# Attention feeding a SwiGLU block: six edits of order in the first 150 microseconds

## The chip, the cores and the metric

The kernel runs on one core of a Trainium2 chip. The time is the device time of one execution in microseconds, given as the median of several runs; less is better. Engines are named as in the profile: PE (TensorE, matmuls), PEld (its weight loads), DVE (VectorE), ACT (ScalarE), POOL (GpSimd) and SP (SyncE, which issues transfers). Each engine runs its own instructions in the order in which they are written, and waits for others through semaphores. A transfer is issued by one engine and lands later, on the 16 DMA engines.

## What is computed

```python
# q, k, v: (8, 12, 448, 64)
scores = scale * np.matmul(q, k.transpose(0, 1, 3, 2))
attn   = softmax(scores)                       # over the last axis
x      = np.matmul(attn, v)                    # (8, 12, 448, 64)
x      = x.transpose(0, 2, 1, 3).reshape(3584, 768)
g      = x @ w_gate                            # (768, 1536)
val    = x @ w_val
out    = (g * sigmoid(g) * val) @ w_out        # (3584, 768)
```

So there are 96 attention heads, taken as 48 pairs (0 to 47), six pairs to a batch entry, and then a gated feed-forward block over 3584 tokens.

## The kernel before

**Pairs.** A pair goes through these stages: its q and k are loaded (`load_qk16`, issued by POOL) and turned to `qkT`; its scores are computed in units (`qk`, PE into a two-bank score tile `s`), exponentiated by ACT into `E`; its v is loaded (`load_v`, POOL) and copied by DVE into `vo` (`copy_v`, L189); the products with v go to `acc` (`pv`, L354/L362 for pairs 0 to 11, L389 for later ones); DVE divides by the sums (R, L373/L414, and xt, L375/L415); and `turn_x` brings xt into X, on PE for pairs 0 to 11 (L447, with a DVE cast at L454), by transposing transfers afterwards.

The turning of q and k changes with the pair: up to pair 10 it is done on PE (`turn`, L262 to L272, 18 transposes into a tile `tp` and a DVE copy); from pair 11 (`NPE`) on POOL copies the raw values (L208) and SP issues two transposing transfers (L210 and L214). `QUAD` is 12: from pair 12 on, scores are cut in another way (L298 for whole units, L310 for the unit RU that two pairs share). `FIRST` is 6 and `WIDE` is 8.

**Feed-forward.** Tokens are cut into blocks, two to a pair of batch entries: even ones with 384 tokens, odd ones with 512. Each block has 12 steps. A step (class `Step`) has six gate matmuls (L519 into `gp`), ACT's Tanh (L544), DVE's `t` (L567), six value matmuls (L519 into `vp`) and DVE's `hts` (L572), the input of the output products. The output products follow: for blocks 0 and 1 plain ones (L606), for later ones groups that use seven products in place of eight (`out_group`, L635), which need sums of weights (L491 to L494, `wsums`, 12 DVE operations) and of `hts` (L502 to L505). The sums wait in a list, `sums`, and `add_sum` issues them one by one at places written by hand.

**PSUM.** There are two rings: `ps_s`, three tiles of two banks, for scores, gates and groups, and `ps_f`, two tiles of one bank, for products, turned values, value matmuls and plain outputs. A gate takes the first bank of a `ps_s` tile and keeps the second as `spare`; in a *bare* visit (below) it takes a `ps_f` tile instead (`gate_small`).

**Order.** The order on each engine is the order in which the code issues instructions. After the first 24 units of scores, the code walks through `plan`, a list of visits. A visit has two or three units of scores (two up to unit 32, three afterwards) and the pairs whose products are due (`todo`). A visit in which none is due is *bare*. In a visit, in this order: the scores; early v copies; for each pair entered, `lead`, the pairs whose copy and transposes (`prep`) are issued, then the loads of a pair 6 further on and of the v of a pair 3 further on; the products; then the v copies of the pairs due in the next visit; then feed-forward work, as much as `run_budget` gives (the time left, over the visits left, plus what was carried); then the turns of the pairs of this visit. `run_budget` takes single steps (`run_fv`), output products (`run_o`) or, in odd blocks, two steps at a time (`run_pair`). In `run_pair` both gates come first, then the first step's value matmuls, then the second step's, in two halves of 256 columns (`split`): the first half goes to `spare`, the bank beside the second step's own gate, so the scheduler lets it start only when `t` of that step has read the gate. From block 2 on, the visits follow the lists `EVEN` and `ODD`.

The early entries to know: entering pair 9 issues the copies of pairs 12 and 13 on POOL; entering pair 10 issues that of pair 14, entering 11 that of pair 15, and entering 10 also the loads of pair 16 and of v of pair 13.

The step 0 of block 0 has one more peculiarity: the sixth of its six input parts comes from the pair 5, whose turn (`late`) is put inside the step, between the first five gate matmuls and the first five value matmuls.

Lines that the change and the prediction touch: `turn` L262, `gate` L527, `value` L547, `run_fv` L800, `run_pair` L811, `run_o` L836, `run_group` L845, `run_budget` L867, `lead` L989, `carry` L1021.

Of the kernel before, what the change touches and what calls it, by code (L numbers as in the profile page):

```python
# [10 lines left out]
FP32 = mybir.dt.float32  # L11
# [12 lines left out]
FIRST = 6  # L24
WIDE = 8
# [7 lines left out]
QUAD = 12  # L33
# [6 lines left out]
def kernel(  # L40
# [16 lines left out]
    NCB = DM // 128  # L57
# [31 lines left out]
    ps_f = ctx.enter_context(tc.tile_pool(name="ps_f", bufs=2, space=PSUM))  # L89
# [129 lines left out]
    def prep(pr):  # L219
        if pr >= QUAD:  # L220
            return prep_quad(pr)
        rq, rk = raw[pr]
        if pr == 0 or pr >= NPE:
            qk16 = attp.tile([128, 2, NC, 2, D], FP16, tag="qk16", name="qk16", bufs=3)[0:P]
            for t, src in enumerate((rq, rk)):
                dst = qk16[:, 1 - t].rearrange("p c h d -> p h c d")
                if pr == 0:
                    nc.vector.tensor_copy(dst[:, 0], src[:, 0])
                    nc.scalar.activation(dst[:, 1], src[:, 1], AF.Copy)
                else:  # L230
                    nc.gpsimd.tensor_copy(dst, src)
        qkT[pr] = attp.tile([128, 2 * S + D], FP16, tag="qkT", name="qkT", bufs=QB)
        if pr >= NPE:
            nc.sync.dma_start_transpose(
                qkT[pr][:, 0 : 2 * S].rearrange("p (c q) -> p c q", q=P),
                qk16.rearrange("p t c h d -> p (t c h d)"),
            )
            nc.sync.dma_start_transpose(
                qkT[pr][:, 2 * S :].rearrange("p (c q) -> p c q", c=1),
                qk16[0:D, 1, 0].rearrange("p h d -> p (h d)"),  # L240
            )
            return None

        def turn0():
            for t in range(2):
                tp = ps_s.tile([128, 2, 512], FP32, tag="s", name="tp")
                for c in range(NC):
                    for hx in range(2):
                        nc.tensor.matmul(
                            tp[ts(hx, 64), c // 2, ds(c % 2 * P, P)],  # L250
                            lhsT=qk16[:, 1 - t, c, hx],
                            rhs=ident[0:P, 0:P],
                            start=True,
                            stop=True,
                        )
                dst = qkT[pr][:, ts(1 - t, S)].rearrange("p (a x) -> p a x", a=2)
                nc.vector.tensor_copy(dst[:, 0], tp[:, 0, 0 : 2 * P])
                nc.scalar.activation(dst[:, 1], tp[:, 1, 0 : 2 * P], AF.Copy)
                if t == 0:
                    nc.vector.tensor_copy(qkT[pr][:, 2 * S :], tp[:, 0, 0:D])  # L260

        def turn():  # L262
            if pr < FIRST + 3:
                tp = ps_s.tile([128, 2, 1024], FP16, tag="s", name="tp")[:, 0]
            else:
                tp = ps_f.tile([128, 1024], FP16, tag="f", name="tp")
            for i in range(2 * NC + 1):
                t, c = (1 - i // NC, i % NC) if i < 2 * NC else (0, 0)
                for hx in range(2):
                    src = raw[pr][t][:, hx, c, :]  # L270
                    nc.tensor.transpose(tp[ts(hx, 64), ts(i, P)], src, ident[0:P, 0:P])
            nc.vector.tensor_copy(qkT[pr][:], tp[:, 0 : 2 * S + D])  # L272

        return turn if pr else turn0
# [207 lines left out]
    gate_small = [False]  # L482
# [25 lines left out]
    class Step:  # L508
# [18 lines left out]
        def gate(self):  # L527
            n = self.at[2]
            if gate_small[0]:
                gate_small[0] = False  # L530
                gp = ps_f.tile([128, 512], FP32, tag="f", name="gp")
            else:
                gs = ps_s.tile([128, 2, 512], FP32, tag="s", name="gp")
                gp, self.spare = gs[:, 0], gs[:, 1]
            if self.late:
                self.vp = ps_f.tile([128, 512], FP32, tag="f", name="vp")
                self.group("g", gp, range(NCB - 1))
                self.late()
                self.group("v", self.vp, range(NCB - 1))
                self.group("g", gp, [NCB - 1])  # L540
            else:
                self.group("g", gp, range(NCB))
            self.sg = fp.tile([128, 512], FP32, tag="sg", name="sg")
            nc.scalar.activation(self.sg[:, 0:n], gp[:, 0:n], AF.Tanh, scale=0.5)  # L544
            self.gp = gp
# [157 lines left out]
    with tc.manual_schedule():  # L703
# [91 lines left out]
        def add_sum(n=1):  # L795
            for _ in range(n):
                if sums:
                    sums.pop(0)()

        def run_fv(quiet=False):  # L800
            step = fvq.pop(0)
            step.gate()
            step.value(0)
            if not quiet:
                add_sum()
            step.finish()
            if not quiet:
                add_sum()
            return 2 * step.time

        def run_pair(small=0):  # L811
            one, two = fvq.pop(0), fvq.pop(0)
            two.split = two.at[2] == 512
            one.gate()
            two.gate()
            one.value(0)
            one.gated()
            if small:
                add_sum()
            two.gated()  # L820
            one.finish()
            two.value(0)
            if not small:
                add_sum()
            two.finish()
            return 4 * one.time
# [9 lines left out]
        def run_o():  # L836
            gen, t = oq.pop(0)
            next(gen)
            if len(oq) < 2 and not groups and wsums:
                sums.extend(wsums[:3])  # L840
                wsums[:3] = []
                add_sum(3)
            return t

        def run_group(nf, inside=None, gate_first=False):  # L845
            gen = groups.pop(0)[0](gate_first)
            for _ in range(nf - 1):
                run_fv()
            step = fvq.pop(0)
            if gate_first:  # L850
                step.gate()
                add_sum()
            next(gen)
            if not gate_first:
                step.gate()
                add_sum()
            if inside:
                inside()
                next(gen)
            step.value(0)  # L860
            add_sum()
            step.finish()
            if not inside:
                next(gen)
            add_sum()

        def run_budget(budget):  # L867
            while (fvq or oq) and budget > 0:
                if not fvq:
                    budget -= run_o()  # L870
                elif len(fvq) > 1 and fvq[0].at[1] and 2 * fvq[0].time < budget <= 4 * fvq[0].time:
                    budget -= run_pair(1)
                else:
                    budget -= run_fv()
            return budget

        def left():
            return sum(2 * step.time for step in fvq) + sum(t for _, t in oq)
# [77 lines left out]
        for x, (chunks, todo) in enumerate(plan):  # L956
# [29 lines left out]
                copy_v(p0)  # L986
            entered = [pr for pr, c in chunks if c == 0]
            for pr in entered:
                lead = [pr + 3] if pr + 3 < QUAD else [pr + 3, pr + 4] if pr + 3 == QUAD else [pr + 4]  # L989
                for p in lead:  # L990
                    if NPE <= p < NPAIR:
                        prep(p)
                if 14 <= pr + LA < NPAIR:
                    load_qk16(pr + LA, 1)
                if 12 <= pr + 3 < NPAIR:
                    load_v(pr + 3)
# [18 lines left out]
            if adds[max(y for y in adds if y <= x)] < 2:  # L1015
                if bare and oq and not fvq:
                    carry -= run_o()
                elif bare:
                    gate_small[0] = True
                out_small[0] = not fvq and bool(oq) and any(p0 >= QUAD for _, p0 in todo)  # L1020
                carry = run_budget(left() / (end - x) + carry)  # L1021
            else:
                nf, ng, no = steps.pop(0) if steps else (0, 0, 0)
                gate_small[0] = bare
                after_group = ng > 0
                if ng:
                    run_group(nf, gate_first=bare)
                    nf = 0
                if no or bare_next(x):
                    for _ in range(nf):  # L1030
                        run_fv()
                else:
                    run_steps(nf)
                for _ in range(no):
                    run_o()
# [55 lines left out]
```

## Time and profile before

| what | before |
|---|---|
| median of 3 runs | 440.3 us (440.25 to 440.62) |
| the profiled execution | 440.02 us |
| its span | 438.3 us |
| PE busy | 429.2 us (98%) |
| DVE, ACT, POOL busy | 260.7, 222.6, 183.0 us |
| PE busy from 0 to 130 us | 125.16 us |
| granted TensorE clock | 1.00 |

The span is the time between the first and the last instruction of the profiled execution; the execution lasts 1.7 us longer. A line of the timeline gives the start and the length in microseconds, the engine, the line of the code, the operation, the tiles that it writes and reads, their shapes, how many instructions it joins, and in brackets the idle time ahead of it with what ended it. On PE the matmuls overlap, so the length of a group has the filling of the array in it, and an idle time in brackets is less than the time lost. At full clock a matmul passes 2.4 columns per ns: one of 384 columns takes 0.16 us, one of 512 takes 0.21.

### The profile page before, as it was taken

To read this page: it belongs to the slowest core of one execution; us is meant where nothing else is said; L and a number is where in the kernel's file an instruction comes from. 1 tells how busy PE (TensorE), PEld (TensorE's weight loads), DVE (VectorE), ACT (ScalarE), POOL (GpSimd) and SP (SyncE) were. 2 spreads that over 40 slices of the span, in tenths; PEclk is the share of its full clock that TensorE was granted. 3 is DMA by queue.
4 is the path that set the end of the run, shared out by engine and by line. 5 is a ranking of instruction groups with operands and counts; after the bars stand their busy time and mean duration, and the time that the engine had idled before them with its cause. 6 is when DMAs were issued, how large, how long until landed. Compare 5 with 4: busy or idle time off the path is not lost.

```text
span 438.3 us, 11082 instructions
## 1 busy us (share of the span) xinstructions
PE 429.2 (98%) x4488; PEld 277.1 (63%) x4488; DVE 260.7 (59%) x604; ACT 222.6 (51%) x332; POOL 183.0 (42%) x301
## 2 busy tenths in 40 slices
PE   8999999999999999999999999999999999999996
PEld 3665556554556676674656676674756778566486
DVE  4666662667668656755456755664556765654562
ACT  6975667546554645464645454546464542222221
POOL 8755624998796446546433553723000000000000
PEclk9999999999999999999999999999999999999999
DMA  9999999999999697965797679964152012202015
GB/s 138 183 199 200 198 175 174 141 159 227 142 144 109 83 167 110 173 81 78 120 140 111 81 125 135 145 103 72 34 107 56 12 30 75 75 2 72 2 36 147
DMA packets 108436, 49.98 MB, mean 114 GB/s; under 512 B 60832, under 2 KB 105024, under 8 KB 108384
## 3 DMA queue, kind: packets, MB, share of 16 engines
q0 software_dynamic: 46928, 24.75, 47.5%
q1 hardware_dynamic: 61296, 24.32, 28.6%
q8 instruction: 35, 0.57, 0.5%
q10 hardware_dynamic: 160, 0.20, 0.1%
q14 instruction: 17, 0.14, 0.1%
HBM read 49.55 MB, written 11.01 MB: 138 GB/s over the span
## 4 chain that ended last, share of the span: by engine, by line
PE 75%; DMA 15%; POOL 4%; DVE 2%; ACT 2%; issue 1%; SPq 0%; DVEq 0%; POOLq 0%
PE gp L519 22%; PE vp L519 19%; PE og L635 17%; PE acc L389 8%; DMA qkraw<-in_k_dram 6%; PE s L298 5%; DMA wg<-in_moe_w_gate_dram 4%; PE op L606 3%; DMA qkraw<-in_q_dram 3%; POOL qkraw L171 2%; DMA qkT<-qk 1%; PE s L310 1%; DVE t L567 1%; ACT E L318 1%; ACT sg L544 1%
## 5 line engine op out<-in xcount | busy, mean ns | idle before, releaser
L318 ACT ACTIVATE E<-s 128x896 f16<-128x896 f32 x126 | 106.6, 918 | 33.5 <-PE s L298 20.2
L519 PE MATMUL gp<-X,wg 128*128 128x384 f16 (+1 forms) x576 | 123.3, 353 | 0.0
L519 PE MATMUL vp<-X,wv 128*128 128x384 f16 (+2 forms) x576 | 120.8, 347 | 0.0
L544 ACT ACTIVATE sg<-gp 128x384 f32<-128x384 f32 (+1 forms) x96 | 52.4, 546 | 89.6 <-PE gp L519 85.2
L567 DVE SCALAR_TENSOR_TENSOR t<-sg,gp 128x384 f32<-128x384 f32 (+1 forms) x96 | 59.5, 620 | 63.4 <-ACT sg L544 62.6
L519 PEld LDWEIGHTS <-wv 128*128 128x128 f16 x606 | 59.2, 98 | 51.6 <-issue 2.0
L519 PEld LDWEIGHTS <-wg 128*128 128x128 f16 x576 | 53.6, 98 | 45.6 <-issue 2.4
L208 POOL COPY qk<-qkraw 128x512 f16<-128x512 f16 x72 | 44.4, 655 | 88.3 <-DMA qkT<-qk 87.7
L572 DVE SCALAR_TENSOR_TENSOR hts<-t,vp 128x384 f16<-128x384 f32 (+2 forms) x96 | 58.2, 607 | 9.9 <-PE vp L519 2.0
L596 POOL DMA_DIRECT2D out_dram<-osb x2 | 1.1, 552 | 131.5 <-DVE osb L688 131.5
L148 POOL DMA_DIRECT2D vraw<-in_v_dram x72 | 44.2, 641 | 9.1 <-DMA wo<-in_moe_w_out_dram 7.5
L148 POOL DMA_DIRECT2D qkraw<-in_k_dram x70 | 42.5, 624 | 6.9 <-DMA wo<-in_moe_w_out_dram 5.6
L635 PEld LDWEIGHTS <-hts 128*128 128x128 f16 x528 | 44.0, 98 | 1.3 <-issue 0.3
L389 PEld LDWEIGHTS <-E 128*128 128x128 f16 (+1 forms) x1152 | 37.4, 96 | 11.1 <-issue 4.6
L336 ACT ACTIVATE E<-s 112x896 f16<-112x896 f32 x48 | 40.7, 917 | 7.3 <-PE s L328 7.1
L389 PE MATMUL acc<-vo,E 128*128 128x65 f16 (+1 forms) x1152 | 42.2, 192 | 0.2 <-DVE hts L572 0.2
L654 ACT ACTIVATE osb<-og 128x384 f32<-128x384 f32 x22 | 10.8, 490 | 44.8 <-PE og L635 40.8
L414 DVE RECIPROCAL R<-acc 128x4 f32<-128x4 f32 x72 | 12.8, 178 | 33.5 <-PE acc L389 33.5
L415 DVE TENSOR_TENSOR xt<-acc,R 128x256 f16<-128x256 f32 x72 | 30.6, 425 | 2.7 <-DMA qkT<-qk 0.3
L171 POOL DMA_DIRECT2D qkraw<-in_q_dram x44 | 30.0, 681 | 3.8 <-DMA wg<-in_moe_w_gate_dram 1.0
L298 PE MATMUL s<-qkT 64*128 64x448 f16 x216 | 30.0, 353 | 0.2 <-DVE t L567 0.2
L635 PE MATMUL og<-wo,hts 128*128 128x192 f16 x264 | 29.0, 246 | 0.0
(81 smaller groups left out, 417.5 us busy)
## 6 DMA issues: line engine op xcount, KB each, us to landing
vraw<-in_v_dram POOLq DMA_DIRECT2D x72, 64.0 KB, 4.3
qkraw<-in_q_dram POOLq DMA_DIRECT2D x41, 112.0 KB, 4.2
qkraw<-in_k_dram POOLq DMA_DIRECT2D x68, 64.0 KB, 4.4
wg<-in_moe_w_gate_dram POOLq DMA_DIRECT2D x8, 288.0 KB, 9.4
wv<-in_moe_w_val_dram POOLq DMA_DIRECT2D x8, 288.0 KB, 10.4
wo<-in_moe_w_out_dram POOLq DMA_DIRECT2D x2, 1152.0 KB, 19.8
out_dram<-osb SPq DMA_DIRECT2D x7, 288.0 KB, 4.1
out_dram<-osb SPq DMA_DIRECT2D x6, 336.0 KB, 4.1
```

What stands on the lines that cost most here:

```text
L148: eng.dma_start(dst[ts(s, 64)], rows)
L171: nc.gpsimd.dma_start(dst, flat.rearrange("h (p c) d -> p h (c d)", c=NC))
L208: nc.gpsimd.tensor_copy(dst.rearrange("p c h d -> p h c d"), src)
L298: nc.tensor.matmul(s[:, hx, 0:S], lhsT=t[ts(hx, 64), ts(c + low(pr, hx), 128)], rhs=t[ts(hx, 64), ds(NC * 128, S)], start=True, stop=True,)
L318: nc.scalar.activation(e[:, 0 : 2 * S].rearrange("p (h q) -> p h q", h=2), s[:, :, 0:S], AF.Exp, scale=sm_scale)
L336: nc.scalar.activation(e[:, :, 0:S], s[0:P, :, 0:S], AF.Exp, scale=sm_scale)
L389: nc.tensor.matmul(acc[:, ts(j, D + 1)], lhsT=e[rows, ds(hx * S + j * 128, 128)], rhs=Vts[pr % NV][rows, hx, col, 0 : D + 1], start=first, ...
L519: nc.tensor.matmul(dst[:, 0:w], lhsT=wslice(kind, self.fb, cb), rhs=X[kk][:, cb, ds(c0 + lo, w)], start=(cb == 0), stop=(cb == NCB - 1),)
L544: nc.scalar.activation(self.sg[:, 0:n], gp[:, 0:n], AF.Tanh, scale=0.5)
L567: nc.vector.scalar_tensor_tensor(self.t1[:, 0:n], self.sg[:, 0:n], 1.0, self.gp[:, 0:n], ALU.add, ALU.mult)
L572: nc.vector.scalar_tensor_tensor(self.hts[:, self.fb, ds(lo, w)], self.t1[:, ds(lo, w)], 0.5 * HS, vp[:, 0:w], ALU.mult, ALU.mult)
L635: nc.tensor.matmul(dst, lhsT=lhs(n), rhs=rhs(n), start=first and n == 0, stop=n == NH - 1, skip_group_check=True)
```

## The change

The whole diff:

```diff
         def turn():
-            if pr < FIRST + 3:
+            if pr < WIDE + 2:
                 tp = ps_s.tile([128, 2, 1024], FP16, tag="s", name="tp")[:, 0]
             else:
                 tp = ps_f.tile([128, 1024], FP16, tag="f", name="tp")
...
             if gate_small[0]:
                 gate_small[0] = False
-                gp = ps_f.tile([128, 512], FP32, tag="f", name="gp")
+                gp, self.spare = ps_f.tile([128, 512], FP32, tag="f", name="gp"), None
             else:
                 gs = ps_s.tile([128, 2, 512], FP32, tag="s", name="gp")
                 gp, self.spare = gs[:, 0], gs[:, 1]
             if self.late:
                 self.vp = ps_f.tile([128, 512], FP32, tag="f", name="vp")
                 self.group("g", gp, range(NCB - 1))
+                self.group("v", self.vp, range(2))
                 self.late()
-                self.group("v", self.vp, range(NCB - 1))
+                self.group("v", self.vp, range(2, NCB - 1))
                 self.group("g", gp, [NCB - 1])
...
         def run_pair(small=0):
             one, two = fvq.pop(0), fvq.pop(0)
-            two.split = two.at[2] == 512
+            two.split = two.at[2] == 512 and not gate_small[0]
             one.gate()
             two.gate()
+            two.spare = one.spare
             one.value(0)
             one.gated()
...
             gen, t = oq.pop(0)
             next(gen)
             if len(oq) < 2 and not groups and wsums:
-                sums.extend(wsums[:3])
-                wsums[:3] = []
-                add_sum(3)
+                n = 3 if oq else 4
+                sums.extend(wsums[:n])
+                wsums[:n] = []
+                add_sum(n)
             return t
...
             step.value(0)
-            add_sum()
             step.finish()
             if not inside:
                 next(gen)
...
-                    budget -= run_fv()
+                    budget -= run_fv(bool(fvq[0].at[1]))
             return budget
...
             for pr in entered:
-                lead = [pr + 3] if pr + 3 < QUAD else [pr + 3, pr + 4] if pr + 3 == QUAD else [pr + 4]
+                lead = {QUAD - 3: [QUAD, QUAD + 1], QUAD - 2: [QUAD + 2, QUAD + 3], QUAD - 1: []}.get(
+                    pr, [pr + 3] if pr < QUAD else [pr + 4]
+                )
...
                 out_small[0] = not fvq and bool(oq) and any(p0 >= QUAD for _, p0 in todo)
-                carry = run_budget(left() / (end - x) + carry)
+                extra = 2 * fvq[0].time if bare and len(chunks) == 3 and fvq and not fvq[0].at[1] else 0
+                carry = run_budget(left() / (end - x) + carry + extra) - extra
```

In words, and in the order of time:

- *Late turn.* In step 0 of block 0, two of the five early value matmuls are issued ahead of the turn of pair 5, three behind it.
- *Pair 9.* The transposes of pair 9 go into a score tile (`ps_s`) instead of a `ps_f` tile.
- *Extra step.* A bare visit of three units while block 0 has steps left gets one more step's time than its share, and gives it back afterwards. There is one such visit; the next one has one step fewer.
- *Copy of pair 15.* Entering pair 10 now issues the copies of pairs 14 and 15, ahead of the loads of pair 16 and of v of pair 13, and entering pair 11 issues none. On POOL the two copies of pair 15 come ahead of five loads; the order of the transfers among each other, on POOL and on SP, is as before.
- *Split value group.* In `run_pair` the second step's first half is written to the bank beside the first step's gate. In a bare visit, where the first gate has no second bank, the second step is not split.
- *Fewer sums.* A single step of an odd block in `run_budget` issues no sums; a group issues one sum fewer in its step's middle; and the last plain output of a block issues four weight sums instead of three.

## The prediction

> **What bounds the kernel now.** First the page's engine rows and the chain that ended last.
>
> ```profile
> PE 429.2 (98%) x4488; PEld 277.1 (63%) x4488; DVE 260.7 (59%) x604; ACT 222.6 (51%) x332; POOL 183.0 (42%) x301
> PE 75%; DMA 15%; POOL 4%; DVE 2%; ACT 2%; issue 1%; SPq 0%; DVEq 0%; POOLq 0%
> ```
>
> PE is busy 98%, so an edit can only win a gap of PE, or matmuls. By windows PE is busy 125.16 of the first 130 us, and from there on nearly always: what is gained or lost before 130 reaches the end undiminished. So I read PE's timeline for its gaps, and the other engines beside each. Ten matter here.
>
> ```profile
> 43.13 0.63 PE L271 MATMUL tp<-ident,qkraw 112*64 112x112 f16 x18 [0.20 <-DVE hts L572]
> 56.09 0.34 PE L354 MATMUL acc<-vo,E 112*128 112x65 f16 x6 [0.42 <-DVE t L567]
> 84.78 0.38 PE L310 MATMUL s<-qkT 64*64 64x448 f16 x3 [0.50 <-DMA qkT<-qk]
> ...
> 90.59 0.81 PE L519 MATMUL gp<-X,wv 128*128 128x256 f16 x6
> ...
> 104.21 0.37 PE L298 MATMUL s<-qkT 64*128 64x448 f16 x2 [0.22 <-DVE t L567]
> ...
> 143.51 0.66 PE L635 MATMUL og<-qkraw,hts 128*128 128x192 f16 x6
> ```
>
> The bracket understates a gap, since starts are pipelined. I take start to start, less the columns at 2.4 per ns: 0.36 us at 43.13, 0.58 at 56.09, 0.54 at 84.78, 0.28 at 90.59 (its twins at 97.69, 108.68, 115.78, 127.61 have the same), 0.39 at 104.21, 0.31 at 143.51.
>
> POOL's and DVE's timelines hold what the change risks.
>
> ```profile
> 68.41 0.60 POOL L148 DMA_DIRECT2D qkraw<-in_k_dram  x1
> 74.57 0.59 POOL L148 DMA_DIRECT2D qkraw<-in_k_dram  x1 [5.55 <-DMA wo<-in_moe_w_out_dram]
> 75.32 1.18 POOL L148 DMA_DIRECT2D vraw<-in_v_dram  x2 [0.17 <-issue]
> 76.49 1.18 POOL L208 COPY qk<-qkraw 128x512 f16<-128x512 f16 x2
> ```
> ```profile
> 81.49 0.46 DVE L189 COPY vo<-vraw 128x512 f16<-128x512 f16 x1
> 81.87 0.55 DVE L491 TENSOR_TENSOR E<-wo 128x768 f16<-128x768 f16 x1
> ...
> 84.71 0.56 DVE L492 TENSOR_TENSOR E<-wo,E 128x768 f16<-128x768 f16 x1
> 86.27 0.18 DVE L414 RECIPROCAL R<-acc 128x4 f32<-128x4 f32 x1 [1.00 <-PE acc L389]
> ...
> 101.57 1.99 DVE L493 TENSOR_TENSOR E<-wo 128x768 f16<-128x768 f16 x1
> ```
>
> POOL waits here for transfers queued behind the weights `wo`, and v of pair 13 (issued 75.32 and 75.90) is asked for ahead of the copy of pair 15 at 76.49.
>
> **The change, part by part. Late turn:** two value matmuls (2 x 0.16) go ahead of the turn at 29.87. But the gate's sixth matmul, 30.86, stays behind that turn's DVE cast, 30.25 to 30.81, so the gap moves from the one place to the other. Bounds: 0 to 0.31 (the gap at 29.40). I take 0.
>
> **Pair 9's transpose in a score bank.** It no longer waits for the value bank that `hts` (42.53 to 43.08) frees; the bare gate behind it, in a value bank, does. That gate starts at 43.43 instead of 43.70: 0.27 won. Its DVE copy at 43.80 is not moved.
>
> **Two steps in the bare visit.** One block-0 step moves from the visit at 57.05 to that at 52.88, and its 12 matmuls stand ahead of the scores at 54.93. The 0.58 at 56.09 goes. The moved step's value bank waits for `t` at 55.48, though, behind the copy of v that took 2.16 (53.22), held beside four POOL copies (52.96, 2.27). If those copies fall as before, since they follow a DMA, the wait is 0.7 and both edits together win 0.13 at the turn of 60.95; if the v copy takes 0.28, as at 56.61, they win 0.78. Later gains are capped: the v of pair 12 lands at 77.02, and DVE's copy and cast end at 78.40, ahead of the products at 78.45. With the slack there, 0.13 to 0.44 is left.
>
> **Copy of pair 15 ahead of pair 16's loads.** The copy needs pair 15's k, which lands at 75.84 behind `wo`. Before, loads 16 (67.76, 68.41, 74.57) and v13 (75.32, 75.90) were issued meanwhile. After, POOL stands from 67.8 to 75.84 and everything behind it waits: copy 15 runs at 76.03, 0.46 earlier, its two transposes go out on SP at 76.68 and 77.97, then q16 at 77.14, two of k16 (77.79, 78.37) and v13 at 78.95 and 79.54: 3.6 later. All five loads move, and what comes behind them on POOL is 2.6 to 3.8 late until about 105. Pairs from 16 on have over 9 us between landing and use, v14 and later likewise, so that lag costs nothing by itself; SP has nothing else there until 81.27.
> The gain: pair 15's second transpose landed at 84.73 (issued 78.43, 6.31 in the chain); 0.46 earlier is 84.27, and PE comes for it at 83.5 to 83.8.
> The price: when v13 lands, V. By the trace's packets, loads issued at 78.83, 79.41 and 80.00 before landed at 84.64, 85.31 and 85.57, across a stretch from 82.4 to 83.6 where the DMA view falls to 42, 26 and 17 GB/s; those at 77.60 and 78.25 landed ahead of it, in 3.9 and 3.65. So V lies between 83.4 (79.54 + 3.9) and 85.1 (85.57 - 0.46). I take 84.3, the middle.
> DVE executes in order. `copy_v(13)`, formerly at 81.49, waits for V, and behind it stand the weight sums, now seven (`run_o` adds four at its last instead of three), then pair 13's R and xt, which free the value banks, then the next visit's t, sum, t and three hts. Copy 0.46, seven sums at the 0.567 pitch (81.87 to 85.27 holds six) 3.97: R at V + 4.45, banks at V + 5.1, and by DVE's own rows (0.69, 0.55, 0.69, 0.69, 0.42, 0.42 with their gaps) the second product bank of pair 14 at V + 9.15, where before had 92.79. At 84.3 that is 0.7 late; at 83.4 0.2 early; at 85.1 1.5 late. The gains above are inside that number, for DVE's chain decides there and PE waits.
> The sums themselves: copy 17 of POOL, formerly 84.75, comes to about 87.4, into their middle. Rows: one sum took 1.99 beside a POOL copy (101.57; 1.42 too much); the sums at 84.71 and 89.16 took 0.56 and 0.55, and the POOL copies beside them (84.75, 89.23) 1.55 and 1.50 instead of 1.18. So 0 to 1.42; I take 0.5, a third, since one meeting of three held DVE.
>
> A page of the Trainium skill, "SBUF — State Buffer", section "SBUF: two separate sides", says that DVE and GpSimd share one port pair as an exclusive lock, taken by whoever starts first for the whole instruction, by a DVE operation with two SBUF inputs too when GpSimd reads SBUF. That speaks against the change: two POOL copies of 0.57 among seven sums would then hold them up by up to 1.2, and the sum below would come out 0.7 worse; the row at 89.16 agrees if DVE came first, the one at 101.57 does not by its start times.
>
> **Split value beside the first gate.** The spare bank is now that of `one`, so the second step's first half waits for t(one), which at 95.65 to 96.34 is done 1.1 before PE could start the half (97.41), not for t(two) (89.85 to 90.54, PE at 90.59). It saves 0.28 at 97.69, 115.78 and 127.61; the one at 90.59 is inside the late chain and counts nothing. The bare visit at 108.68 is no longer split: 12 matmuls fewer, 0.26. The bank of `one` stays held until the first half's `hts` (98.54 to 98.96 there), and its next user, the second score tile, comes 0.2 behind the first at 99.09: hidden by 0.3, and if not, some 0.1 to 0.3 each.
>
> **Fewer sums.** The sum at 101.57 goes from ahead of t: 0.39 at 104.21. The one at 141.10 goes behind `osb`: 0.31 at 143.51. Where sums now meet (148.60 and its like in two later blocks), t comes 0.33 later, about 0.1 each on the third score bank: 0 to 0.3; I take 0.1. The other stall in view, 122.50, waits for hts and stays.
>
> **The sum.** Late chain 0.7 + 0.5, sums meeting 0.1; off go 3 x 0.28 + 0.26 + 0.39 + 0.31 = 1.8. That is -0.5 on the profiled execution's 440.02: 439.5. The median is 440.3, 0.28 above; 439.8 for a median.
>
> **Rivals. v13 comes early.** If the slow stretch of the DMA is not there, V is 83.4 and the late chain nothing (-0.2, no hold): -1.9, 438.4. For it: loads at 77.60 and 78.25 took under 4; against: the stretch followed an instruction fetch of PE at 81.53, which after has too.
> **v13 late and sums held (slower).** One place, DVE from 81.5 to 90: V at 85.1 (+1.5), the sums held by the whole 1.42, and 0.3 for sums that meet: 3.2 - 1.8 = +1.4, 441.7. It decides from the point where V's lateness and the hold exceed 2.6 together (1.8 + 0.88). For it: 6.31 for the transpose at 78.43, and the copy of v at 53.22, held 1.9 by POOL; against: 89.16.
> **The gaps only move.** The split gains need t(one) to be the last thing waited for. If the 512-wide hts of `one` or a bank takes its place, 1.1 of the 1.8 is gone: +0.6, 440.9. Against: DVE has idle time of 0.2 to 0.9 in each of these visits.
>
> **How the numbers follow.** What a measurement of this kernel can tell from no change is 0.2%, 0.88 us. The forecast (V from 83.9 to 84.9, hold up to 0.9) has 0.45 and its own range 439.1 to 440.7; a third of it lies below 439.42. Early v13 0.28, all faster. Late and held 0.22, all but 0.02 slower. Gaps that move 0.05, the same but for 0.03. Faster 0.43, same 0.34, slower 0.23. The range, 438.1 to 441.5, leaves out the ends of the second and third case.
>
> **What would show it.** Right: POOL's copy at about 76.0, v13's copy on DVE ending 84.4 to 85, no 0.50 at L310 or less of it, a gap of PE ahead of the value matmuls near 89 that is new, and the 0.28 gaps gone. Wrong: v13's copy before 83.6 or after 85.2; a sum above 1 us between 85 and 89; split halves that still wait for t; a new gap of PE after 130.

## The result, and the profile after

| | before | after |
|---|---|---|
| median | 440.27 us (440.13 to 440.62, 6 runs) | 442.77 us (441.99 to 443.95, 6 runs) |
| ratio | | 1.0056, 95% interval 1.004 to 1.0072 |
| profiled execution (its span) | 440.02 (438.3) | 441.99 (440.2) |

The change makes the kernel 2.5 us slower; the forecast was 0.5 less, and the range ended at 441.5. The profiled execution is the fastest of the six, so its trace shows 1.97 of the 2.5. The page's engine rows and the chain that ended last, after:

```profile
PE 429.5 (98%) x4482; PEld 276.3 (63%) x4482; DVE 257.0 (58%) x603; ACT 222.7 (51%) x332; POOL 183.1 (42%) x301
PE 76%; DMA 13%; POOL 4%; DVE 3%; issue 3%; ACT 1%; DVEq 0%; POOLq 0%
```

They say little: PE's work is the same, and the difference is gaps. PE's timeline after, where the gaps are:

```profile
84.43 0.38 PE L310 MATMUL s<-qkT 64*64 64x448 f16 x3 [0.48 <-DMA qkT<-qk]
...
85.76 1.13 PE L389 MATMUL acc<-vo,E 64*128 64x65 f16 x32 [0.47 <-DVE vo L189]
86.73 2.75 PE L519 MATMUL gp<-X,wg 128*128 128x512 f16 x12
91.37 1.47 PE L519 MATMUL vp<-X,wv 128*128 128x512 f16 x6 [1.88 <-DVE xt L415]
93.00 0.82 PE L519 MATMUL gp<-X,wv 128*128 128x256 f16 x6 [0.16 <-DVE t L568]
...
100.16 0.82 PE L519 MATMUL gp<-X,wv 128*128 128x256 f16 x6
```

Pair 13's products wait for the copy of its v (85.76), and the value matmuls at 91.37 wait for DVE's xt of that pair. POOL's timeline after, at the place that is reordered, and DVE's beside it:

```profile
67.70 1.17 POOL L208 COPY qk<-qkraw 128x512 f16<-128x512 f16 x2 [0.77 <-issue]
76.39 1.17 POOL L208 COPY qk<-qkraw 128x512 f16<-128x512 f16 x2 [7.52 <-DMA qkraw<-in_k_dram]
...
79.32 1.22 POOL L148 DMA_DIRECT2D vraw<-in_v_dram  x2
...
88.50 1.86 POOL L208 COPY qk<-qkraw 128x512 f16<-128x512 f16 x2
```
```profile
85.11 0.60 DVE L189 COPY vo<-vraw 128x512 f16<-128x512 f16 x1 [3.77 <-DMA vraw<-in_v_dram]
85.63 0.54 DVE L491 TENSOR_TENSOR E<-wo 128x768 f16<-128x768 f16 x1
...
87.34 0.78 DVE L492 TENSOR_TENSOR E<-wo,E 128x768 f16<-128x768 f16 x1
88.04 0.96 DVE L491 TENSOR_TENSOR E<-wo 128x768 f16<-128x768 f16 x1
89.11 0.78 DVE L492 TENSOR_TENSOR E<-wo,E 128x768 f16<-128x768 f16 x1
89.81 0.96 DVE L493 TENSOR_TENSOR E<-wo 128x768 f16<-128x768 f16 x1
90.69 0.17 DVE L414 RECIPROCAL R<-acc 128x4 f32<-128x4 f32 x1
```

POOL stands 7.52 us before copy 15, and v of pair 13 is asked for at 79.32 and 79.90 instead of 75.32 and 75.90. By the trace's packets it lands at 84.67 and 85.02. DVE stands 3.77 us for it, then does the copy and seven sums, and only at 90.69 pair 13's R, which had been at 86.27. Four of the sums are longer, 0.78 to 0.96 instead of 0.55: three of them overlap POOL's copies at 88.50, and the first, at 87.34, ends before those start. The seven take 5.14 us instead of 7 x 0.567 = 3.97.

Now both profiles are followed along PE, the start of each group after against its start before. After is 2.35 late at the value matmuls (91.37 against 89.02), 2.62 at the products of pair 14 (95.19 against 92.57), and 2.75 at the gate behind them. Then it wins 0.28 at each split visit (three), 0.39 near 104 and 0.28 in the bare visit, and loses 0.26 behind that: 1.51 late at block 2's first gate (132.18 against 130.67). It wins 0.30 more near 143, and loses 0.34 at 253.46 and 0.34 at 297.77. With some hundredths elsewhere that makes 1.97, the difference of the profiled executions. Of the last two losses, the first is the sums again: a sum of 0.85 beside a POOL copy, and `t` behind it.

```profile
252.10 0.85 DVE L505 TENSOR_TENSOR qkraw<-hts,hsum 128x768 f16<-128x768 f16 x1
...
253.46 0.36 PE L298 MATMUL s<-qkT 64*128 64x448 f16 x2 [0.17 <-DVE t L568]
```

The gap at 297.77, behind a late `osb` of DVE, is also in the profile of the split group alone, which is faster than before; its cause is open.

### The profile page after: what moved, and what is told of

Read it like the earlier page. It is cut to its first block, busy times and chain, and to the rows that moved or that the text cites. A ratio compares the mean times of both kernels' runs of the same rounds, so it can differ in the third digit from the quotient of the medians.

```text
span 440.2 us, 11071 instructions
## 1 busy us (share of the span) xinstructions
PE 429.5 (98%) x4482; PEld 276.3 (63%) x4482; DVE 257.0 (58%) x603; ACT 222.7 (51%) x332; POOL 183.1 (42%) x301
## 4 chain that ended last, share of the span: by engine, by line
PE 76%; DMA 13%; POOL 4%; DVE 3%; issue 3%; ACT 1%; DVEq 0%; POOLq 0%
PE gp L519 22%; PE vp L519 20%; PE og L636 17%; PE acc L389 7%; PE s L298 5%; DMA qkraw<-in_k_dram 4%; DMA wg<-in_moe_w_gate_dram 4%; DMA qkraw<-in_q_dram 3%; PE op L607 3%; POOL qkraw L171 2%; DMA vraw<-in_v_dram 1%; PE s L310 1%; POOL qk L208 1%; POOL vraw L182 1%; ACT E L318 1%
```

## The experiments

All times are medians, each beside runs of the kernel before on the same chip.

| kernel | this | before | ratio, 95% interval | lowest to highest |
|---|---|---|---|---|
| the change without the reordering on POOL | 439.55 | 440.38 | 0.9984 (0.9972 to 0.9996) | 438.79 to 440.95 |
| before, with the reordering alone | 442.22 | 440.38 | 1.0041 (1.0029 to 1.0054) | 441.87 to 442.39 |
| the change, v13 loaded first | 442.48 | 440.38 | 1.0037 (1.0012 to 1.0062) | 438.97 to 444.41 |
| the change, copy of v13 behind the sums | 443.06 | 440.38 | 1.0059 (1.0035 to 1.0083) | 440.36 to 445.39 |
| the change, X of pair 17 first on SP | 442.29 | 440.46 | 1.0040 (1.0022 to 1.0058) | 440.95 to 443.82 |
| the change, v13 and X first | 439.13 | 440.46 | 0.9972 (0.9952 to 0.9993) | 437.61 to 442.17 |
| without the reordering, X first | 440.16 | 440.46 | 0.9990 (0.9977 to 1.0003) | 438.42 to 440.99 |
| before, X first | 440.24 | 440.46 | 0.9997 (0.9984 to 1.0010) | 439.26 to 441.14 |
| before, split group alone | 439.12 | 440.32 | 0.9971 (0.9958 to 0.9983) | 438.34 to 440.51 |
| before, fewer sums alone | 441.09 | 440.32 | 1.0013 (0.9999 to 1.0027) | 440.56 to 442.42 |
| copy of v13 behind the sums, X first | 440.83 | 440.32 | 1.0017 (0.9999 to 1.0035) | 439.61 to 443.56 |
| before, the three early edits alone | 440.69 | 440.32 | 1.0004 (0.9990 to 1.0018) | 439.61 to 441.44 |
| before, reordering with v13 and X first | 440.03 | 440.67 | 0.9989 (0.9977 to 1.0002) | 439.26 to 441.50 |
| the same with the split group | 439.22 | 440.67 | 0.9964 (0.9948 to 0.9980) | 437.62 to 440.76 |
| the change, v13 and X first, sums as before | 438.41 | 440.67 | 0.9953 (0.9940 to 0.9967) | 437.56 to 440.28 |

**Take the reordering out, and put it in alone.**

```diff
-                lead = {QUAD - 3: [QUAD, QUAD + 1], QUAD - 2: [QUAD + 2, QUAD + 3], QUAD - 1: []}.get(
-                    pr, [pr + 3] if pr < QUAD else [pr + 4]
-                )
+                lead = [pr + 3] if pr + 3 < QUAD else [pr + 3, pr + 4] if pr + 3 == QUAD else [pr + 4]
```

> The change without its reordering on POOL: the loads of pair 16 and of v of pair 13 go ahead of the copy of pair 15 again, all else as changed. Theory A (the loss is the late v of pair 13, with the weight sums queued behind it on DVE): v lands at about 78.8 again, the gap of 2.05 us ahead of the value matmuls near 89 and the one of 0.63 at 85.76 go, and the gains of the other edits stay: 1.0 to 2.0 us less than before, 438.3 to 439.3 as a median, and the runs lie within 0.5 us of each other again. Theory B (the loss is made by the moved step or the sums, and v is only in the same place): 441 or more.

Measured 439.55 against 440.38, 0.8 less than before: just outside the first theory's bounds (1.0 to 2.0 less), and far from the second's. The gap at 91.37 is gone (value matmuls at 89.45). The scatter did not shrink as expected: 2.2 us.

The reverse edit on the kernel before:

> The kernel before with the reordering on POOL alone. Theory A: v of pair 13 lands at about 85, six sums (3.4 us, and up to 1.2 more beside POOL's copies) stand behind it on DVE, and the second product bank of pair 14 comes at V + 8.6 + 0 to 1.2, where before had 92.79: 0.8 to 2.0 us late, 441.1 to 442.3. Theory B: 440.0 to 440.6.

442.22, 1.84 more, within the first theory's bounds. So the reordering alone is slower than before, and it is what makes the change slow: with it 1.0056, without it 0.9984. This is shown; how it does it took the next runs.

**Mend its first cost: v13 first.**

```diff
                 for p in lead:
+                    if p == 15:
+                        load_v(13)
                     if NPE <= p < NPAIR:
                         prep(p)
...
-                if 12 <= pr + 3 < NPAIR:
+                if 12 <= pr + 3 < NPAIR and pr != 10:
                     load_v(pr + 3)
```

> The change with the two loads of v of pair 13 put ahead of the copy of pair 15, those of pair 16 behind it as changed. Theory A: v lands at about 77 to 78, no queue behind it, and what is left of the reordering is harmless: as the run without the reordering, 438.3 to 439.3, within 0.3 us of it. If it is the copy 15 or the later loads of pair 16 that hurt, it stays above 440.5.

A miss: 442.48, and the runs spread over 5.4 us. In its profile v13 lands at 77.73, the largest gap of PE between 79 and 108 is 0.3 (at the shared unit near 84), and PE begins block 2's first gate 2.51 ahead of before (128.16 against 130.67): all gains are there. And then they are lost at this gate. PE's timeline of this run at that gate and the granted clock of its page (40 slices of 11 us, in tenths), PE's timeline of the kernel before at the same place, and SP's timeline of this run and, last line, of the kernel before:

```profile
128.16 0.98 PE L519 MATMUL gp<-X,wg 128*128 128x384 f16 x5
131.98 0.43 PE L519 MATMUL gp<-X,wg 128*128 128x384 f16 x1 [2.84 <-DMA X<-xt]
132.20 2.12 PE L519 MATMUL vp<-X,wv 128*128 128x384 f16 x6
PEclk9999999999998999999999999999999999999999
```
```profile
130.67 1.14 PE L519 MATMUL gp<-X,wg 128*128 128x384 f16 x6
131.65 1.14 PE L519 MATMUL vp<-X,wv 128*128 128x384 f16 x6
```
```profile
122.00 1.21 SPq L456 DMA_TRANSPOSE X<-xt  x1
123.26 2.06 SPq L460 DMA_TRANSPOSE X<-xt  x1
125.44 1.20 SPq L210 DMA_TRANSPOSE qkT<-qk  x1
126.75 1.25 SPq L214 DMA_TRANSPOSE qkT<-qk  x1
128.54 1.19 SPq L456 DMA_TRANSPOSE X<-xt  x1
```
```profile
123.91 1.19 SPq L456 DMA_TRANSPOSE X<-xt  x1
```

The gate's sixth matmul needs X of pair 17, a transposing transfer that SP issues at 128.54 and that lands at 131.94. The kernel before issues it at 123.91, and it lands at 128.58, 2.9 ahead of need. SP is nearly back to back here, mostly 1.2 to 1.3 us for each transpose, and in its order X of pair 17 stands behind two qkT transposes. The lateness began with POOL's stand of 7 us: in this profile the next copies are at 84.12 and 88.55, where before had 80.58 and 84.75, and the transposes behind them go out on SP at 84.76 and 89.25 instead of 81.27 and 85.77. From about 93 SP has hardly any idle time in which to catch up: 3.5 us late at first, it is 4.6 late at X of pair 17. So the lateness on POOL, which the prediction took for harmless, goes on to SP, and from there to PE forty microseconds later.

The wait itself is 3.01 us, start against start (PE would have come to the sixth matmul at 128.97). Behind it PE runs slowly: the next six value matmuls take 2.12 where before took 1.14, and the granted clock is 0.53, 0.50, 0.50 and 0.76 in the four microseconds from 132 to 136. That is 1.7 us of full clock lost on top of the wait, and 0.4 more in a wait for `hts` at 139.88, so that 2.51 ahead has become 2.55 behind at the first group (140.83 against 138.28). None of the other sixteen profiles has a lowered clock ahead of the last 2 us of its span, and in none does PE stand for as long behind the start (2.30 in brackets at most). That the wait lowers the clock is likely from this, but one profile alone shows it.

This bears on the scatter. Each execution has its mean granted clock on record. In this run the seven longest executions (442.42 to 444.41) have 0.992 to 0.996, the five others (438.97 to 441.41) 0.998 to 1.000. The lowered stretch of the profile accounts for 0.004 of that mean (1.7 of 441 us).

**Mend the sums' place instead: copy of v13 behind them.**

```diff
-                if p0 not in early:
+                if p0 not in early and p0 != 13:
                     copy_v(p0)
...
                 carry = run_budget(left() / (end - x) + carry + extra) - extra
+                if 13 in vcopies.get(x, []):
+                    copy_v(13)
```

> The change with DVE's copy of v of pair 13 put behind the seven weight sums instead of ahead of them; v is as late as in the change. Theory A with both halves (late v and the sums behind it): the sums run from 81.4 while v is on its way, end at about 85.4 to 86.5, the copy follows, pair 13's R comes at about 86.8 to 87.5 instead of 90.69: 3 to 4 us earlier at R, and the time 438.8 to 440.0. If lateness of v alone made the loss, the time stays within 0.7 us of the change's 442.8.

443.06, which by the expectation's letter says that lateness alone makes the loss. The profile says otherwise: R of pair 13 comes at 87.69, 3.0 earlier than in the change and close to what was expected, and the gap near 91 is gone, though 1.82 is left ahead of pair 13's products. PE begins block 2's first gate at 130.88, only 0.2 behind before, and there the same new wait, 2.27 for X of pair 17, makes most of the loss.

**Put X of pair 17 ahead.** On SP, the two transposes of qkT that are issued in the visit of pair 17's products go behind its X:

```diff
+            hold[0] = any(p0 == 17 for _, p0 in todo)
...
                 else:
                     turn_x(p0)
+            while behind:
+                behind.pop(0)()
...
+        behind.append(transposes)
+        if not hold[0]:
+            while behind:
+                behind.pop(0)()
```

(`transposes` holds the two transfers of L210 and L214.)

> The change with one thing moved on SP: the two transposing transfers of X of pair 17, which block 2's first gate needs, go ahead of the two of qkT that stand before them. Theory C: the reordering has a second cost, by way of SP: POOL is some 2 to 4 us late, so the qkT transposes are, and X of pair 17 stands behind them in SP's order; block 2's first gate then waits for X in some executions (3.01 us in the run with v first, 2.27 in the run with the copy behind the sums, none in the profile of the change). X comes 2.6 us earlier (two transposes of 1.3), so the slow executions go: 441.5 to 442.3 as a median, spread under 1 us where the change had 442.0 to 444.0. If the spread has another cause, it stays at 2 us, and the median at 442.5 to 443.2.

> The run with v of pair 13 first, with X of pair 17 ahead on SP too. Theory C: the wait of 3.01 us at block 2's first gate shrinks to 0 to 0.5, all else stays: 442.8 - 2.5 to 3.0 in a profile like that one, 438.5 to 440.0 as a median, with a spread below 2 us instead of 5.4. Against it: 441.5 or more, and the wait of the same length.

> The run without the reordering on POOL, with X of pair 17 ahead on SP. Theory C: the wait of 0.47 at block 2's first gate goes: 438.6 to 439.3. The run without it had 439.55. Against it: no difference.

> The kernel before with X of pair 17 ahead on SP alone: there X lands 2.9 us before PE needs it, so nothing is to be won: within 0.5 us of before. If it gains more than 0.7, X was late in some runs of before as well.

With v first it is decisive: 442.48 becomes 439.13. SP and PE in that run:

```profile
123.30 1.81 SPq L464 DMA_TRANSPOSE X<-xt  x1
125.16 1.22 SPq L468 DMA_TRANSPOSE X<-xt  x1
126.49 1.19 SPq L464 DMA_TRANSPOSE X<-xt  x1
```
```profile
128.06 1.12 PE L397 MATMUL acc<-vo,E 64*128 64x65 f16 x32
129.01 1.14 PE L527 MATMUL gp<-X,wg 128*128 128x384 f16 x6
```

X goes out at 126.49, and the six gate matmuls run without a wait. The spread is still 4.6 us, where less than 2 was expected: two of the twelve executions are above 441 (441.60 and 442.17), and these two alone have a mean clock below 0.998 (0.996 and 0.995). In the change itself X first gave little: 442.29, intervals overlapping. Its spread is 2.9: its six shorter executions (440.95 to 442.03) have a mean clock of 0.998 to 1.000, its six longer ones (442.54 to 443.82) 0.994 to 0.996. The profiled one is a shorter one, so where the clock fell is not on record. In the change v13 holds PE back by 2.6, and X has that much more time. The two costs lie behind each other: mending X alone is worth little, mending v alone hands the gain to the wait for X and the lowered clock behind it, and mending both is worth 3.7 us (1.0056 to 0.9972 of 440.3). With X first in both, v first takes the change from 1.0040 to 0.9972, intervals well apart: so the late v is shown to be the first cost. Without the reordering X first made no difference (0.9984 and 0.9990, a miss: 0.3 to 0.9 less was expected), and none in the kernel before, as expected.

> The run with DVE's copy of v of pair 13 behind the seven sums, with X of pair 17 ahead on SP. Theory A and C together: the first cost of the reordering is v late with the sums behind it (the gap ahead of the value matmuls is gone in the run with the copy behind, but 1.82 is left where pair 13's products wait for the copy), the second is X of pair 17 (2.27 there). So the second goes, the first is 1.2 smaller than in the change: 440.0 to 441.3, against 443.06 without X ahead and 442.3 for the change with X ahead. If the sums' place did not matter: 442 or more.

440.83, 2.2 less than without X first and within the bounds. That the sums ahead of R are a part of the first cost is likely from this and from R's time in the profile; it is not shown, since the interval overlaps that of the change with X first (1.0040, 1.0022 to 1.0058). A wait of 1.52 for X is left in this profile even so.

**The other parts alone.**

> The kernel before with the split value group beside the first gate alone. By the prediction's step: 0.28 saved at each of four visits, 0.26 in the bare visit, less 0.24 for the wait that the whole value group of the bare visit brings (the change's profile has it at 112.45): 1.1 less, 439.0 to 439.7, where before has 440.4; in the profile no gap ahead of the split halves. If the gaps only move: 440.2 to 440.6.

The edit is that of `run_pair` and `gate` as in the diff. 439.12, 1.2 less, as expected; PE's timeline has no gap ahead of the split halves (90.70, 97.53), and 0.26 where the bare visit's whole value group is waited for.

> The kernel before with fewer sums alone. By the prediction's step: 0.39 and 0.31 gone, 0.1 or so back at each of three places. The change's profile has 0.34 at 252.94 instead and the run without the reordering 0.56 at 149.87, so: between 0.4 less and 0.3 more, 440.0 to 440.7.

The edits of `run_o`, `run_group` and `run_budget` as in the diff. 441.09 against 440.32: above the bounds; from no change to 1.2 slower by the interval, and not the 0.6 gain of the prediction. The profile shows where the 0.39 near 104 went. DVE's and ACT's timelines of this run in the bare visit that follows:

```profile
107.08 0.69 DVE L567 SCALAR_TENSOR_TENSOR t<-sg,gp 128x512 f32<-128x512 f32 x1 [2.10 <-ACT sg L544]
...
108.16 0.68 DVE L567 SCALAR_TENSOR_TENSOR t<-sg,gp 128x512 f32<-128x512 f32 x1
```
```profile
104.03 2.54 ACT L318 ACTIVATE E<-s 128x896 f16<-128x896 f32 x3 [1.05 <-PE s L310]
106.43 1.33 ACT L544 ACTIVATE sg<-gp 128x512 f32<-128x512 f32 x2
```

ACT does three exponentials from 104.03 and the two Tanh behind them without a pause, so t of the second step ends at 108.84 though PE lost nothing at 104. The gap ahead of the split half there is 0.63 instead of 0.28: most of the 0.39 moved 4 us on. Nor is the 0.39 found in other profiles with the old places of the sums: before with X first has no gap at 104 and 0.84 at the later place, the early edits alone have none and 0.99, and the split group alone has none at 104 either.

> The kernel before with the three early edits alone (late turn, pair 9 in a score bank, one step more in the bare visit). By the prediction's step 0.1 to 0.4 of what they win is left behind 78: 440.0 to 440.3; PE is about 0.9 ahead at the turn near 61. If the transposes of pair 15 (a gap of 0.67 to 1.37 at the shared unit near 84 in these runs) decide instead, nothing is left: 440.4.

440.69 against 440.32, no difference: 0.87 is won at the turn near 61 (61.09 against 61.96), and at the shared unit near 84 PE waits 1.55 for the transposes of pair 15 and resumes at 85.13. Without the reordering that unit resumed between 84.78 and 85.46 in every profile, with it between 84.43 and 84.75, or the unit ran on with 0.4 lost at most: these transposes, not the v of pair 12 alone, cap what is won ahead of them.

**What is left of the reordering, freed of its costs.**

> The kernel before with the reordering alone, but v of pair 13 loaded ahead of the copy of pair 15 and X of pair 17 ahead on SP. If v and X are the whole cost of the reordering, what is left is the gain it gives at the shared unit near 84 (PE resumes at 84.4 to 84.6 with it and at 84.8 to 85.5 without it): 0.3 to 0.9 less than before, 439.4 to 440.1, where the reordering alone had 442.22. If it has a third cost, 441 or more.

> The same with the split value group beside the first gate: the two gains add, 1.2 and 0.3 to 0.9: 438.2 to 438.9. If they do not add (another wait takes over), 439.1 as the split group alone.

> The run with v and X first, with the sums where the kernel before had them. If fewer sums cost what they showed alone (0.7, with an interval from 0 to 1.2), 438.0 to 439.1, and no gap near 250; if they cost nothing or gain by the prediction's step (0.6), 439.1 to 439.8.

The reordering with v and X first: 440.03 against 440.67, 0.6 less, with an interval that ends at no change. So no cost of the reordering is left once v and X go first (1.0041 becomes 0.9989). With the split group 1.45 less: a miss, above the bounds and less than the sum of the two, and one wait of 2.10 for X is in its profile. The change with v and X first and the old places of the sums is the fastest kernel here: 438.41 against 440.67, ratio 0.9953 (0.9940 to 0.9967), and its profile has no gap near 250, both as expected. Against the same kernel with fewer sums (0.9972, 0.9952 to 0.9993) the intervals overlap, so that the sums cost something is possible, but not shown.

## Why the prediction was wrong, by its own steps

- **Copy of pair 15, the late chain.** This is the step that failed for the number: the sum had 0.7 + 0.5 = 1.2 for it, and it measured 2.6 (2.75 with the gap at the next gate). The mechanism, the place and the formula were right, two inputs were mis-sized. V, the landing of v13, was put at 84.3 and was 85.02 (the upper bound was 85.1); the hold of the sums was put at 0.5 and was 5.14 - 3.97 = 1.17. By the prediction's own V + 9.15 + hold the second bank comes at 95.34; pair 14's products start at 95.19 on the first. The late chain makes 1.5 of the 2.5 between the -0.5 of the sum and the +1.97 of the profile. Of the rest, 0.6 is the two gaps at 253.46 and 297.77, where the sum had 0.1, and 0.2 the bare visit. The rival v13 late and sums held, 441.7, is the one that came true, and the median was 1.1 above it. Two of the prediction's own signs of being wrong are there: v13's copy ends at 85.71, after 85.2, and there are new gaps of PE after 130.
- **"Pairs from 16 on have over 9 us between landing and use, v14 and later likewise, so that lag costs nothing by itself."** This step was wrong as well, though the profile of the change shows no loss by it. It counted the slack of the transfers that POOL issues, and not what stands behind their copies on SP. X of pair 17 does, in the middle of a stretch where SP issues nearly back to back. In that profile v13 holds PE back further; the cost appears as soon as v13 is mended (3.01, and 1.7 by the clock behind it).
- **The gain of copy 15.** The transposes went out at 77.03 and 78.31 and the second landed at 84.39, near the 84.27 forecast; PE still waited 0.48 in brackets. Over all profiles the second lands at 83.73 to 84.71 with the reordering (ten), at 84.73 to 85.42 without (seven): it does bring it forward, by some tenths.
- **Split value group.** Forecast 1.1; alone 1.2. Right. Missed: the 0.26 wait for the whole value group in the bare visit.
- **Fewer sums.** Forecast 0.6 of gain; alone no gain (0.0 to 1.2 lost). The 0.39 stood behind one sum of 1.99 in the one profiled execution; it is absent from other profiles with the old places of the sums, and behind it comes a visit bound by ACT that takes such a gain over. Of the "0.1 each" where sums meet, one measured 0.34 (253.46) and one 0.56 (149.87, without the reordering), each behind a sum lengthened to 0.85 or 1.06.
- **Early edits.** Forecast 0.1 to 0.4 left; alone none shown. The cap named, v of pair 12, is there, but pair 15's transposes cap it once more. That the late turn wins nothing was right (the gap is now at 30.44, 0.32 in place of the 0.31 at 29.87).
- **The rule on the shared port pair** ("SBUF — State Buffer", section "SBUF: two separate sides" of the Trainium skill). It spoke against the change with up to 1.2 of hold, and 1.17 was measured, so the trace agrees in size. It agrees less in detail: the three sums that overlap POOL's copies took 0.78 to 0.96 and the copies 1.86 instead of 1.18, so both sides lost, and the lengthened sum at 87.34 lies ahead of the copies.

## What to carry to other kernels

A copy moved ahead of transfers on an in-order queue delays all that the queue issues, and what stands behind those copies on the next queue; follow the lateness through every queue until a place with real slack, not to the first. Where two waits lie behind each other, mending one shows no gain: read the profile of the mended kernel before dropping the theory. Read the granted clock behind a long wait of PE too: here 1.7 us followed a wait of 3.0. A gap of a few tenths in one profiled execution, caused by one lengthened instruction, is not a gain to be had until other profiles show it too and the engine behind it has been shown to have room.

## What was not expected of the hardware

SP took 1.2 to 1.3 us for most transposing transfers, now and then 1.8 to 2.8, and from about 105 to 135 us it issued them with hardly a pause: in this stretch SP, which has no row among the page's engines, set when X came. The landing times of the same transfers moved from run to run (without the reordering, the second transpose of pair 15 released PE anywhere from 84.8 to 85.5). In the run with v first a stretch of 3.4 us at half the granted clock followed PE's wait of 3.01, and the three kernels that spread over more than 4 us (v13 first, copy of v13 behind the sums, v13 and X first) all have executions with a mean clock of 0.996 or less. Those of the change itself are not all explained by it: of its six, only the one of 443.13 has a low mean clock (0.995), the two longest have 0.999 and 1.000.
